# Chunk 0 of a fused scan and MLP kernel: state sums moved to other PSUM banks, halves copied first, two unused products on TensorE ahead of the sums

## The chip, the cores and the metric

The kernel runs on one core of a Trainium2 chip. The metric is the device time of one execution in microseconds, as the median over runs. A core has a matrix engine (TensorE, "PE" in the profile, its weight loads "PEld"), a vector engine (VectorE, "DVE"), a scalar engine (ScalarE, "ACT"), GpSimd ("POOL"), and SyncE ("SP"), which issues most DMAs. Each engine works through its own list of instructions in order and waits on semaphores for the others. PE writes its results to PSUM, here eight banks of 128 partitions x 512 float32 values; DVE and ACT read them there.

## The reference

Two computations follow each other. The first is a state-space scan over 4 batches, 8 heads and 768 tokens, with head size 32 and state size 16, here in chunks:

```python
cum = np.cumsum(la, axis=-1)                       # la = log(clip(a))
L = np.exp(cum[:, :, :, None] - cum[:, :, None, :]) * causal
M = np.einsum('bhin,bhjn->bhij', Cc, Bc) * L
y = einsum(M, xc) + einsum(Cc, state) * exp(cum)
state = exp(sum(la)) * state + sum_j(B_j x_j * exp(cum_last - cum_j))
```

The second takes y as 3072 tokens of 256 values and applies an MLP with a hard-swish: `h = y @ w_in` (256 x 2048), `g = h * clip(h + 3, 0, 6) / 6`, `out = g @ w_out` (2048 x 256). The weights come as float64 and are decoded to float32 on the chip.

## The kernel before, in words

**Tiling.** The 768 tokens are six chunks of 128 tokens; a chunk of all four batches is 512 columns of the MLP. Within a chunk the scan works in two halves of 64 tokens. `scores` (line 569) makes C·B for four pairs of heads, each pair q in its own bank `cb` (tags `f0` to `f3`). `multiply` (line 624) multiplies each pair by the decays `L` on DVE (line 637). `into_state` (line 592) makes the sums of B and x over a half: `sps[c][0]` for the first half, `sps[c][1]` for the second. `take` (line 620) copies the second one to `adds` on ACT; for chunk 0 the first one goes to `mid` on ACT, in two copies with a mask (line 632). `mix` (line 673) then makes y: for each half of the heads (u = 0, 1) products of x with `L` (line 685), and for chunk 0 behind each of them the products of `csT` with `mid` (line 556, `from_state`). `keep` (line 694) copies the four parts of y to `yT` on ACT, and `renew` (line 656) makes the next state from `mid` and `adds` on DVE.

**Banks.** `own_banks` (line 561) gives a chunk the two banks `y0` and `y1`. In each the first half of the columns is for y of the first 64 tokens, and the second half is for the sums. `own_halves` (line 665) gives y of the second 64 tokens two more banks, `f0` and `f1`. [...] In chunk 0 `d` (differences of sums of logs, lines 383 to 420) stands in `f0` to `f3` for chunk 0 itself, and for chunk 1 in two `o` banks and in `y0` and `y1`; ACT's exponentials (`diff_exp`, line 422) free them. `diff_mask` (line 385) puts a mask into these banks at the very start with products of up to 512 columns.

**Order.** The order on each engine is written out by hand (line 1155 on; no scheduler moves anything). For chunk 0: logs and differences, `scores(0)`, differences of chunk 1, `own_banks(0)`, `into_state(0, 0, 1)`, `multiply(0)`, `fade`, `mix(0)`, `keep(0)`. Between them stand steps that decode the first of four pieces of w_in (`weights(0, ..)`, lines 235 to 288, DVE and ACT). Loads of weight pieces (`load_w`, line 141) go into three `raw` buffers in turn. Piece 1 is issued by SP once DVE has written one element of its buffer; that write (line 154) stands in `multiply(0)` behind the second product of line 637. Piece 2 follows when piece 1 has landed (line 156). Later pieces wait for a buffer that has been decoded.

**The MLP of chunk 0.** From line 1210, `mlp_in` (line 706) makes 16 blocks of h, each 128 x 512, from two float32 products (line 711) in the banks `f0` to `f3` in turn. ACT makes the ramp (line 814), DVE multiplies it with h (line 819), which frees the bank. Decoding of the next weight pieces stands between these steps on ACT and DVE: block f uses piece f // 4 of w_in. `first_out` (line 822) then makes the output product with w_out, with chunk 1 of the scan in between.

Of the kernel before, what the change touches and what calls it, by code (L numbers as in the profile page):

```python
# [8 lines left out]
FP32 = mybir.dt.float32  # L9
# [12 lines left out]
def kernel(  # L22
# [24 lines left out]
    nc = tc.nc  # L47
    P = 128
    NB, NH, S, D = x.shape
    N = B.shape[-1]  # L50
    DM, DF = moe_w_in.shape[0], moe_w_out.shape[0]
    NC = S // P
# [6 lines left out]
    HT = P // 2  # L59
# [8 lines left out]
    ps = ctx.enter_context(tc.tile_pool(name="ps", bufs=1, space=PSUM))  # L68
# [17 lines left out]
    TURN = 2  # L86
# [54 lines left out]
    def load_w(i, queue=nc.sync):  # L141

        raw = loads.tile([P, NK * FP * 2 * P], U32, name="raw", bufs=NRAW)
        if i < NP:
            cols = slice(2 * i * FP * P, 2 * (i + 1) * FP * P)
            src = moe_w_in[:, cols].rearrange("(k p) f -> p k f", p=P)
            dst = raw.rearrange("p (k f) -> p k f", k=NK)
        else:
            r0 = (i - NP) * FP * P
            src = moe_w_out[r0:r0 + FP * P, :].rearrange("(k p) m -> p k m", p=P)  # L150
            dst = raw.rearrange("p (k m) -> p k m", k=FP)
        raws[i] = raw
        if i == 1:
            nc.vector.memset(raw[:, :1], 0)
        if i == 2:
            nc.gpsimd.tensor_copy(raw[:, :1], raws[1][:, :1])
        queue.dma_start(out=dst, in_=src)
# [6 lines left out]
    ident = const.tile([P, P], FP32, name="ident")  # L164
# [5 lines left out]
    def conceal_in(t, pattern):  # L170
# [23 lines left out]
        out=head, in_=head, pattern=[[-2 * N, NQ], [-N, 2]], compare_op=ALU.is_ge,  # L194
        fill=0.0, base=0, channel_multiplier=1)
    nc.gpsimd.affine_select(
        out=head, in_=head, pattern=[[2 * N, NQ], [N, 2]], compare_op=ALU.is_ge,
# [183 lines left out]
    ys, cbs, sps, adds = {}, {}, {}, {}  # L381
# [3 lines left out]
    def diff_mask(c, b):  # L385

        if c == 0:
            d = ps.tile([P, NH, HT], FP32, name="d", tag=f"f{b}")
        elif b < 2:
            d = ps_o.tile([P, NH, HT], FP32, name="d", tag="o")  # L390
        else:
            d = ps_y.tile([P, NH, HT], FP32, name="d", tag=f"y{b % 2}")
        n = NH if c else NH // (1 if b == 0 else 2 if b == 1 else 4)
        for h in range(0, NH, n):
            nc.tensor.matmul(
                out=d[:, h:h + n], lhsT=ident_h,
                rhs=hide.unsqueeze(1).to_broadcast([P, n, HT]), start=(h == 0), stop=True,
                skip_group_check=True)
        ds[c, b] = d
# [150 lines left out]
    def from_state(c, a, pairs=range(NQ)):  # L550

        csT, state = bTs[c][2], (mids[c] if a else states[c - 1])
        for b in range(NB):
            for q in pairs:
                pair, d0 = slice(32 * q, 32 * q + 32), 2 * D * (q % 2)
                nc.tensor.matmul(  # L556
                    out=ys[c][a, q // 2][d0:d0 + 2 * D, b], lhsT=state[pair, b],
                    rhs=csT[pair, b, HALF[a]], start=(a == 0 and b == 0), stop=True,
                    tile_position=(32 * q, d0), skip_group_check=True)

    def own_banks(c):

        both = [ps_y.tile([P, 2, NB, HT], FP32, name=f"y{u}", tag=f"y{u}") for u in range(2)]
        ys[c] = {(0, u): both[u][:, 0] for u in range(2)}
        sps[c] = [both[a if 0 < c < NC - 1 else 1 - a][:, 1] for a in range(2)]
        if c and c != TURN:
            from_state(c, 0)

    def scores(c):

        bT, cT, _ = bTs[c]
        cbs[c] = [ps.tile([P, NB, 2, HT], FP32, name="cb", tag=f"f{q}") for q in range(NQ)]
        if c not in ys and c:
            own_banks(c)
        for b in range(NB):
            for a, rows in enumerate(HALF):  # L580
                for q in range(NQ):
                    pair = slice(32 * q, 32 * q + 32)
                    nc.tensor.matmul(  # L583
                        out=cbs[c][q][rows, b], lhsT=bT[pair, b, rows],
                        rhs=cT[pair, b, :, rows], start=(b == 0), stop=True,
                        tile_position=(32 * q, a * HT), skip_group_check=True)
        if c == TURN:
            from_state(c, 0)
        if 0 < c <= TURN:
            into_state(c, *range(1 if c == TURN else 2))  # L590

    def into_state(c, *halves):
        xt, bs = xts[c], bss[c]
        own = c > TURN, c >= TURN
        if c > TURN:
            sps[c][0] = ps.tile([P, NB, 2 * D], FP32, name="sp", tag="f3")
        if c == 0:
            one = sps[c][0][:1, 0, :1]
            for left, right in ((ident_h[:, :1], hide[:, :1]), (bs[:, 0, :1], ident[:, :1])):
                nc.tensor.matmul(  # L600
                    out=one, lhsT=left, rhs=right, start=True, stop=True, skip_group_check=True)
        for b in range(NB):
            for q in range(NQ):
                hs = slice(b * NH + 2 * q, b * NH + 2 * q + 2)
                for a in halves:
                    nc.tensor.matmul(
                        out=sps[c][a][32 * q:32 * q + 32, b],
                        lhsT=bs[HALF[a], hs].rearrange("s h n -> s (h n)"),
                        rhs=xt[HALF[a], hs].rearrange("s h d -> s (h d)"),
                        start=(b == 0 and (c == 0 or own[a])), stop=True,  # L610
                        tile_position=(a * HT, 32 * q), skip_group_check=True)

    def new_state(t, sp, old):
        for u in range(2):
            ds_ = slice(u * D, (u + 1) * D)
            nc.vector.scalar_tensor_tensor(
                out=t[:, :, ds_], in0=sp[:, :, ds_], scalar=parity[:, u:u + 1],
                in1=old[:, :, ds_], op0=ALU.mult, op1=ALU.add)

    def take(c):  # L620
        adds[c] = att.tile([P, NB, 2 * D], FP32, name="adds", bufs=1)
        nc.scalar.copy(out=adds[c], in_=sps[c][1])

    def multiply(c):

        if c < TURN:
            take(c)
        if c <= TURN:
            mids[c] = mid = att.tile([P, NB, 2 * D], FP32, name="mid", bufs=1)
        if c == 0:  # L630
            for t in range(2):
                nc.scalar.activation(
                    mid[:, :, t * D:(t + 1) * D], sps[c][0][:, :, t * D:(t + 1) * D], AF.Copy,
                    scale=parity[:, t:t + 1])
        for q in (2, 0, 1, 3) if c >= TURN else range(NQ):
            hs = slice(2 * q, 2 * q + 2)
            nc.vector.tensor_tensor(
                out=Ls[c][:, :, hs], in0=Ls[c][:, :, hs], in1=cbs[c][q], op=ALU.mult)
            if c == 0 and q == 1:
                load_w(1)  # L640
            if 0 < c <= TURN and q == 1:
                new_state(mid, sps[c][0], tmps[c])
# [22 lines left out]
    def own_halves(c, more=0):  # L665

        for u in range(2):
            t = ps.tile([P, 1 + more * (1 - u), NB, HT], FP32, name="y2", tag=f"f{u}")
            ys[c][1, u] = t[:, 0]
            if u < more:  # L670
                ys[c]["more"] = t[:, 1]
# [176 lines left out]
    def weight_sums():  # L848


        t1 = w4[:, 0, 1]
        for n, p_, q_, op in ((3, lambda: w4[:, 1, 1], lambda: t1, ALU.subtract),
                              (2, lambda: wsums[3], lambda: w4[:, 0, 0], ALU.add),
                              (4, lambda: w4[:, 1, 0], lambda: wsums[2], ALU.subtract),
                              (1, lambda: t1, lambda: w4[:, 0, 0], ALU.subtract)):
            pool, tag = {1: (att, "yT"), 4: (const, f"w{NP - 1}")}.get(n, (const, f"t{n}"))
            wsums[n] = pool.tile([P, NJ, P], FP32, name=f"t{n}", tag=tag, bufs=1)
            nc.vector.tensor_tensor(out=wsums[n], in0=p_(), in1=q_(), op=op)
            yield
# [285 lines left out]
    def weights(i, n):  # L1145
        for _ in range(n):
            next(parts[i], None)
# [7 lines left out]
    for c in range(2):  # L1155
        for b in range(NB):
            diff_mask(c, b)
# [24 lines left out]
    for b in range(2, NB):  # L1182
        diff(1, b)
        diff_exp(1, b)
    weights(0, 2)
    own_banks(0)
    into_state(0, 0, 1)
    multiply(0)
    fade(0, HALF[1])
    weights(0, 1)  # L1190
# [16 lines left out]
    for k in range(NC):  # L1207
        gTs[k] = ffn.tile([P, NF, TB], FP32, name="gT")
        c, ahead = k + 1, k + 2
        if k == 0:  # L1210
# [16 lines left out]
            more, ins = weight_sums(), [in_parts(i) for i in range(NP)]  # L1227
# [101 lines left out]
        for i, _ in enumerate(wide_units(k)):  # L1329
# [18 lines left out]
            if c < NC:  # L1348
# [5 lines left out]
                u = {TURN: 7, TURN + 1: 7, TURN + 2: 5}.get(c, 5)  # L1354
# [49 lines left out]
```

## Time and profile before

| what | us |
|---|---|
| median of 3 runs (lowest, highest) | 338.85 (338.52, 339.15) |
| profiled execution, its own time | 339.71 |
| its span, first to last instruction | 338.0 |
| PE busy | 329.5 |
| DVE busy | 263.0 |
| ACT busy | 208.3 |
| POOL busy | 130.8 |
| mean granted TensorE clock | 0.990 of full |

The profile is of one execution. A row of the order of time gives start, length, engine, line, operation, output tile and inputs, form, and count; in brackets stands how long the engine was idle before it and what ended that. Rows of one line that follow each other are merged. A float32 product of PE shows as two records. "PEclk" and the clock column say which share of the full TensorE clock was granted.

### The profile page before, as it was taken

The numbers are of one execution on the slowest core, as the hardware profiler recorded it, in microseconds if no ns is written. First come the engines' busy times: TensorE is split into PE (matmuls) and PEld (weight loads), VectorE is DVE, ScalarE is ACT, GpSimd is POOL, SyncE is SP. The second block draws the span as 40 slices with busy tenths as digits, with TensorE's granted clock in tenths as the row PEclk, the third lists the DMA queues.
The fourth block names the chain that finished last, engine by engine and source line by source line (L and its number), as shares of the span: only waits on it lengthen the run. The fifth ranks groups of instructions, "written<-read, shape, count | busy, mean of one in ns | idle before, by whom it ended". The sixth has DMA issues, their size and how long they took to land.

```text
span 338.0 us, 8336 instructions
## 1 busy us (share of the span) xinstructions
PE 329.5 (97%) x3361; PEld 265.8 (79%) x3361; DVE 263.0 (78%) x419; ACT 208.3 (62%) x450; POOL 130.8 (39%) x126
## 2 busy tenths in 40 slices
PE   7799999999999999999999999999999999999995
PEld 3564448888868888888888888888888888899995
DVE  7778999879699729868959658947668958599974
ACT  3868887658985762587652478634488212677661
POOL 2100000162365699169984068781048750000000
PEclk9959999999999999999999999999999999999999
DMA  6769980492980206229207249100142001110001
GB/s 101 166 205 322 130 326 14 110 138 60 205 110 0 51 19 143 46 44 101 43 2 161 35 64 82 41 4 8 27 64 28 2 4 17 27 21 0 2 0 62
DMA packets 90278, 25.22 MB, mean 75 GB/s; under 512 B 82881, under 2 KB 86625, under 8 KB 89729
## 3 DMA queue, kind: packets, MB, share of 16 engines
q1 hardware_dynamic: 89664, 24.57, 38.5%
q8 instruction: 26, 0.43, 0.5%
q10 hardware_dynamic: 576, 0.13, 0.2%
q14 instruction: 12, 0.09, 0.1%
HBM read 21.33 MB, written 3.29 MB: 73 GB/s over the span
## 4 chain that ended last, share of the span: by engine, by line
PE 82%; DVE 6%; SPq 5%; ACT 2%; POOL 2%; DMA 2%; issue 1%; POOLq 0%
PE h L775 23%; PE h L711 9%; PE o L832 8%; PE wc L1023 7%; PE wb L1023 7%; PE o_end L987 6%; PE wa L1023 6%; SPq L1054 4%; PE wb L1031 3%; PE y L685 3%; PE y L556 2%; DVE q_part L915 2%; DVE gT L819 2%; DMA xt<-in_x_dram 2%; PE cb L583 2%
## 5 line engine op out<-in xcount | busy, mean ns | idle before, releaser
L819 DVE SCALAR_TENSOR_TENSOR gT<-gT,h 128x512 f32<-128x512 f32 x96 | 64.8, 684 | 24.4 <-ACT gT L814 22.9
L814 ACT ACTIVATE gT<-h,half 128x512 f32<-128x512 f32 x96 | 65.4, 686 | 21.8 <-PE h L775 21.2
L795 ACT ACTIVATE h<-h 128x512 f32<-128x512 f32 x66 | 38.3, 586 | 38.1 <-PE h L775 37.9
L775 PE MATMUL h<-y_hi,w_part 128*128 128x512 f32 x160 | 51.7, 408 | 0.6 <-DVE gT L819 0.5
L775 PE MATMUL h<-y_less,w_part 128*128 128x512 f32 x160 | 50.0, 399 | 0.0
L775 PE MATMUL h<-y_lo,w_part 128*128 128x512 f32 x160 | 49.5, 395 | 0.0
L878 POOL TENSOR_TENSOR s<-gT 128x512 f32<-128x512 f32 x16 | 24.9, 1556 | 51.1 <-DVE gT L819 51.1
L775 PEld LDWEIGHTS h<-y_hi,w_part 128*128 128x128 f32 x160 | 29.9, 188 | 7.9 <-DVE gT L819 1.5
L775 PEld LDWEIGHTS h<-y_lo,w_part 128*128 128x128 f32 x160 | 30.0, 188 | 7.3
L775 PEld LDWEIGHTS h<-y_less,w_part 128*128 128x128 f32 x160 | 29.1, 188 | 6.2 <-DVE h L792 0.3
L445 ACT ACTIVATE L<-L,cum_n 128x64 f32<-128x64 f32 x128 | 31.9, 339 | 2.2 <-POOL L L173 2.2
L711 PE MATMUL h<-yT,w_in 128*128 128x512 f32 x64 | 29.4, 622 | 0.0
L832 PE MATMUL o<-w_out,gT 128*128 128x256 f32 x128 | 28.8, 381 | 0.0
L832 PEld LDWEIGHTS o<-w_out,gT 128*128 128x128 f32 x128 | 24.1, 190 | 3.8 <-issue 0.5
L711 PEld LDWEIGHTS h<-yT,w_in 128*128 128x128 f32 x64 | 12.7, 201 | 16.0 <-issue 13.9
L878 POOL TENSOR_TENSOR gT<-gT 128x512 f32<-128x512 f32 x16 | 23.9, 1499 | 0.7
L173 POOL TENSOR_SCALAR_AFFINE_SELECT L<-L 64x1024 f32<-64x1024 f32 (+1 forms) x16 | 19.5, 1229 | 8.4 <-DMA L<-cum_d 8.1
L915 DVE TENSOR_TENSOR q_part<-gT,q_part 128x256 fp32r<-128x256 f32 x24 | 21.4, 922 | 0.0
L987 PE MATMUL o_end<-v_pair,g_pair 128*128 128x256 f32 x120 | 21.0, 281 | 0.0
L878 POOL TENSOR_TENSOR s<-s,gT 128x512 f32<-128x512 f32 x16 | 20.6, 1293 | 0.0
L987 PEld LDWEIGHTS o_end<-v_pair,g_pair 128*128 128x128 f32 x120 | 18.8, 189 | 1.2
L456 POOL TENSOR_TENSOR bs<-B,L 128x128 f32<-128x128 f32 x24 | 11.7, 504 | 18.7 <-ACT L L445 12.7
(170 smaller groups left out, 617.3 us busy)
## 6 DMA issues: line engine op xcount, KB each, us to landing
raw<-in_moe_w_in_dram SPq DMA_DIRECT2D x4, 1024.0 KB
raw<-in_moe_w_out_dram SPq DMA_DIRECT2D x4, 1024.0 KB
L<-cum_d SPq DMA_DIRECT2D x8, 512.0 KB
xt<-in_x_dram SPq DMA_DIRECT2D x6, 512.0 KB
out_dram<-back SPq DMA_DIRECT2D x128, 16.0 KB
B<-in_B_dram SPq DMA_DIRECT2D x6, 256.0 KB
eto<-cum_e SPq DMA_DIRECT2D x20, 64.0 KB
pairs<-in_C_dram SPq DMA_DIRECT2D x36, 32.0 KB
```

The lines of the kernel that those rows point to most:

```text
L173: nc.gpsimd.affine_select(out=t[rows], in_=t[rows], pattern=pattern, compare_op=ALU.is_ge, fill=-1e5, base=base, channel_multiplier=-1)
L445: nc.scalar.activation(Ls[c][:, b, h], Ls[c][:, b, h], AF.Exp, bias=cum_n[:, c, g:g + 1])
L711: nc.tensor.matmul(out=h[:, t:t + n], lhsT=w_in[f // FP][:, j, f % FP * P:(f % FP + 1) * P], rhs=yTs[k][:, j].rearrange("p b i -> p (b i)" ...
L775: nc.tensor.matmul(out=hs_[k, f], lhsT=w[j][:, f % FP * P:(f % FP + 1) * P], rhs=y[:, j], start=(start and j == 0), stop=True, skip_group_ ...
L795: nc.scalar.activation(h, h, AF.Copy, scale=1.0 / EPS + 1.0)
L814: nc.scalar.activation(gTs[k][:, f], h, AF.Relu, bias=half, scale=1.0 / 6.0)
L819: nc.vector.scalar_tensor_tensor(out=g, in0=g, scalar=1.0, in1=h, op0=ALU.min, op1=ALU.mult)
L832: nc.tensor.matmul(out=o[:, b % 2], lhsT=gTs[0][:, f, b * P:(b + 1) * P], rhs=w_out[:, f], start=(f == 0 and b % 2 == 0), stop=True, skip_ ...
L878: nc.gpsimd.tensor_tensor(out=o, in0=p_, in1=q_, op=op)
L915: nc.vector.tensor_tensor(out=l[:, j], in0=g[:, j], in1=h[:, j].bitcast(FP32), op=ALU.subtract)
L987: nc.tensor.matmul(out=ends_["cross" if n == 2 else "squares"][b], lhsT=g_parts[t][n][:, b * P:(b + 1) * P], rhs=w, start=(t == 0 and b < ...
L1023: nc.tensor.matmul(out=bank[:, slot], lhsT=lhs[:, j], rhs=rhs[:, j], start=(clear and j == 0), stop=True, skip_group_check=True)
```

## The change

In chunk 0 alone:

- The state sums go to two banks of their own, `f1` (first half) and `f0` (second half), which held `cb` of pairs 1 and 0. The banks `y0` and `y1` hold y alone.
- The y of the second 64 tokens goes to `f2` and `f3` in place of `f0` and `f1`.
- ACT copies the two masked halves of the first sum (`mid`) before the second sum (`adds`).
- Ahead of the sums, PE makes two float32 products of the identity with itself, repeated to 512 columns, into bank `y0`. Nothing reads them.
- At the start, the mask products of `diff_mask` for batches 2 and 3 of chunk 0 have 256 columns each in place of 128: four products in place of eight.

```diff
@@ diff_mask
-        n = NH if c else NH // (1 if b == 0 else 2 if b == 1 else 4)
+        n = NH if c else NH // (1 if b == 0 else 2)
@@ own_banks
-        sps[c] = [both[a if 0 < c < NC - 1 else 1 - a][:, 1] for a in range(2)]
+        if c:
+            sps[c] = [both[a if c < NC - 1 else 1 - a][:, 1] for a in range(2)]
+        else:
+            sps[c] = [ps.tile([P, NB, 2 * D], FP32, name="sp", tag=f"f{1 - a}") for a in range(2)]
         if c and c != TURN:
             from_state(c, 0)
+        return both[0].rearrange("p t b i -> p (t b i)")
@@ multiply
-        if c < TURN:
+        if 0 < c < TURN:
             take(c)
         if c <= TURN:
             mids[c] = mid = att.tile([P, NB, 2 * D], FP32, name="mid", bufs=1)
...
                     mid[:, :, t * D:(t + 1) * D], sps[c][0][:, :, t * D:(t + 1) * D], AF.Copy,
                     scale=parity[:, t:t + 1])
+            take(c)
@@ own_halves
-            t = ps.tile([P, 1 + more * (1 - u), NB, HT], FP32, name="y2", tag=f"f{u}")
+            t = ps.tile([P, 1 + more * (1 - u), NB, HT], FP32, name="y2", tag=f"f{u if c else 2 + u}")
@@ the order of chunk 0
-    own_banks(0)
+    free = own_banks(0)
+    for _ in range(2):
+        nc.tensor.matmul(
+            out=free, lhsT=ident, rhs=ident.unsqueeze(1).to_broadcast([P, NB, P]),
+            start=True, stop=True)
     into_state(0, 0, 1)
```

## The prediction

> **What bounds the kernel now.** I read the page first, then the chain of waits from 14 to 70 us, then stretches cut at the clock's steps, then the order of time on each engine.
>
> ```profile
> span 338.0 us, 8336 instructions
> PE 329.5 (97%) x3361; PEld 265.8 (79%) x3361; DVE 263.0 (78%) x419; ACT 208.3 (62%) x450; POOL 130.8 (39%) x126
> PEclk9959999999999999999999999999999999999999
> ```
>
> PE (TensorE) is busy for 97% of the span, so the time is PE's work plus its few holes. One digit of the clock row is not 9: the third slice (17 to 25 us), right where the change is made.
>
> ```profile
> 14.11 0.60 ACT L L425
> 16.93 0.27 ACT adds L622
> 17.24 0.96 PE y L685 x53
> 18.20 1.04 PE y L556 x16
> 19.24 1.11 PE y L685 x61
> 20.35 1.05 PE y L556 x16
> 21.40 29.31 PE h L711 x64
> 50.71 13.81 PE o L832 x64
> ```
>
> The chain of chunk 0: it runs on ACT (ScalarE) until 17.2 us, ending in the copy `adds`; then PE makes the second product y in four pieces (4.16 us) and, without a hole, the block product h.
>
> ```profile
> 11.04:14.45 3.41, 3.03 (x115) 2.22 (x115) 2.60 (x5) 2.10 (x3) 0.00 (x0) 1.00 1.24 159
> 14.45:17.86 3.41, 1.69 (x129) 1.43 (x130) 3.41 (x8) 3.23 (x6) 0.00 (x0) 1.00 0.37 68
> 17.86:21.28 3.42, 3.42 (x122) 2.90 (x104) 2.26 (x6) 1.12 (x3) 0.00 (x0) 0.50 0.61 246
> 21.28:24.69 3.41, 3.41 (x8) 1.51 (x5) 2.85 (x7) 3.21 (x6) 0.64 (x1) 0.50 0.48 127
> 24.69:28.10 3.41, 3.41 (x9) 1.52 (x8) 2.69 (x6) 2.33 (x4) 0.00 (x0) 1.00 1.02 400
> 29.03:36.50 7.47, 7.47 (x19) 3.34 (x18) 7.40 (x12) 6.19 (x8) 0.00 (x0) 1.00 1.17 202
> ```
>
> Columns: stretch and length, busy time of PE, weight loads, DVE (VectorE), ACT, POOL, then granted clock, DMA share, GB/s. The clock is halved from 17.86 to 24.69 us, two steps of 3.41 us. The 3.41 us before the drop hold 1.69 us of PE work; the 3.41 us before that hold 3.03, and the clock stayed. The last row: from 29.03 to 36.50 PE and DVE (7.40 of 7.47) are both full.
>
> **The change, part by part.** The rows it touches:
>
> ```profile
> 13.42 1.29 ACT L425 ACTIVATE L<-d 128x512 f32<-128x512 f32 x2 [0.47 <-PE d L417]
> 14.45 1.89 DVE L637 TENSOR_TENSOR L<-L,cb 128x512 f32<-128x512 f32 x3
> 15.54 0.86 PE L606 MATMUL y<-xt,bs 64*32 64x64 f32 x64 [0.57 <-DMA xt<-in_x_dram]
> 15.68 0.06 DVE L154 MEMSET raw<- 128x1 uint32 x1
> 15.78 7.08 SPq L157 DMA_DIRECT2D raw<-in_moe_w_in_dram  x3
> 15.78 1.15 ACT L273 ACTIVATE we<-we,bias_lo 128x1024 uint16<-128x1024 bf16 x1
> 16.25 0.68 DVE L637 TENSOR_TENSOR L<-L,cb 128x512 f32<-128x512 f32 x1
> 16.83 0.35 ACT L622 COPY adds<-y 128x256 f32<-128x256 f32 x1
> 17.09 0.63 ACT L632 ACTIVATE mid<-y,parity 128x128 f32<-128x128 f32 x2
> 17.90 1.22 DVE L287 SCALAR_TENSOR_TENSOR w_in<-wm,we 128x1024 f32<-128x1024 f32 x1
> ```
>
> *Masks at the start.* Eight mask products of 128 columns become four of 256: the same columns, back to back on PE either way. I take 0; it could be a few hundredths either way, hidden by PE's wait for x at 15.54.
>
> *Two idle products.* Each is 128x512 f32, the shape of an L711 product, which PE runs in two halves:
>
> ```profile
> 23.20 0.34 PEld L711 LDWEIGHTS h<-yT,w_in 128*128 128x128 f32 x1 [0.52 <-issue]
> 24.05 0.34 PEld L711 LDWEIGHTS h<-yT,w_in 128*128 128x128 f32 x1 [0.52 <-issue]
> 24.80 0.19 PEld L711 LDWEIGHTS h<-yT,w_in 128*128 128x128 f32 x1 [0.41 <-issue]
> 25.23 0.19 PEld L711 LDWEIGHTS h<-yT,w_in 128*128 128x128 f32 x1 [0.24 <-issue]
> ```
>
> Starts lie 0.85 us apart at half clock and 0.43 at full: one product is 0.86 us warm, two are 1.72. They write the bank that `diff_exp(1, 2)` frees at about 14.06 (the first half of the L425 row: 13.42 plus half of 1.29), so with the first weight load they last until about 15.95. Behind them on PE wait the two one-element products and the sums. Those started at 15.54, when x landed; now about 16.0, 0.46 later. Upper bound, if they run at half clock: 1.7 us more.
>
> *Sums in banks f1 and f0.* A new wait: these banks hold `cb` of pairs 0 and 1 until DVE's first two L637 products, done at 14.45 + 2 x 0.63 = 15.71 (third of 1.89 each). PE is still in the idle products then: 0. Gain: the first y product no longer shares a bank with the sums, so it needn't wait until `adds` has been copied (17.2); it follows the sums on PE at 16.0 + 0.86 = 16.86 instead of 17.24: 0.38 earlier. Its new banks f2 and f3 wait for the third and fourth L637 products; the fourth ends at 16.93, and the half that needs it comes 1.3 us after 16.86. 0.
>
> *Halves first.* ACT is in L273 until 16.93 either way. `mid` (0.63) now goes ahead of `adds` (0.35) and ends near 17.5, when the first quarter of y ends; `adds` then ends near 17.9, and its readers on DVE (`renew`) stand behind L287, which ends at 19.12. 0.
>
> *The clock.* From 14.45 to 17.86 PE would be busy nearly throughout (products until 15.95, sums, y): about 3.3 us against 1.69, more than the 3.03 that kept the clock. I take it that the clock stays. Then y costs, by halving 1.04, 1.11 and 1.05 and with 0.8 for the first piece (the sums, 64 halves of its form, took 0.86 with their end), about 2.4 us in place of 4.16: 1.75 less; h could start near 19.3 instead of 21.4. Its first block, four halves at 0.85, becomes four at 0.43: another 1.7 us. The clock is worth 3.45 us, and PE would be 3.8 us ahead.
>
> ```profile
> PE y L685 <- ACT adds L622: 0.8, 1, 0.8
> ```
>
> This is the longest of PE's holes there (from the waits: in total, times, longest). [...]
>
> *What is late next.* The lead is not kept. PE reuses four banks; block 8 of h needs block 4 multiplied by its ramp on DVE.
>
> ```profile
> 27.29 1.12 ACT L246 COPY ws<-raw 128x1024 uint16<-128x1024 uint16 x1 [1.05 <-DMA raw<-in_moe_w_in_dram]
> 29.03 0.69 DVE L819 SCALAR_TENSOR_TENSOR gT<-gT,h 128x512 f32<-128x512 f32 x1 [1.58 <-ACT gT L814]
> 35.23 1.27 DVE L819 SCALAR_TENSOR_TENSOR gT<-gT,h 128x512 f32<-128x512 f32 x2
> 36.82 0.19 PEld L711 LDWEIGHTS h<-yT,w_in 128*128 128x128 f32 x1 [0.24 <-issue]
> 42.03 1.49 DVE L819 SCALAR_TENSOR_TENSOR gT<-gT,h 128x512 f32<-128x512 f32 x2
> 47.89 1.22 DVE L287 SCALAR_TENSOR_TENSOR w_out<-wm,we 128x1024 f32<-128x1024 f32 x1
> 65.00 0.59 ACT L491 COPY bT<-t_ps 128x512 f32<-128x512 f32 x1 [2.02 <-PE t_ps L482]
> ```
>
> Block 1 starts at 24.80 and a block takes 4 x 0.43, so block 8 starts at 36.82. The L819 product of block 4 is the first of the two at 35.23 and ends at about 35.9: PE has 0.9 us in hand there. DVE got to 35.23 by its own full program since 29.03; that began when ACT had copied the third piece of w_in, whose DMA landed just before 27.29; that DMA follows the second piece's, which SP issued at 15.78 behind the memset at 15.68. Nothing of this row of causes moves with PE: the memset still stands behind the second L637 product. So in the new kernel block 8 starts no sooner than 35.95, however early y is: **the gain is 36.82 - 35.95 = 0.87 us**, and the other 2.9 us become PE holes before it (block 5 too must wait for the L819 of block 1, done at 29.03 + 0.69). The next places have more in hand: block 12 (24.80 + 44 x 0.43 = 43.7) against the first L819 at 42.03, done at 42.7: 0.96; the second matrix at 50.7 against L287's end at 49.11: 1.6. At 65.00 ACT waits for PE, and from there the other engines mostly follow PE, so the 0.87 us should reach the end.
>
> Sum: +0.46 (sums later) is covered by the old wait for `adds`, net -0.38 at y; clock -3.45; given back up to block 8 +2.96; total -0.87. The profiled execution took 339.71 us (span 338.0 and 1.7 around it), 0.86 more than the median of the runs, 338.85; I take the difference off the median: 338.85 - 0.87 = 337.98.
>
> **Rivals.**
>
> *The clock drops anyway.* If what counts is how much of the array works, the small y products weigh little: the stretch from 17.86 to 21.28 had PE busy throughout with them, and the clock didn't come back until 3.41 us of 128x512 products had followed. Against it: from 11.04 to 14.45 PE ran small products too, mixed with some 128x512 ones, and the clock stayed; the idle products are full size. Then y is 0.38 us earlier at half clock and that is worth half after 24.69: 0.19, 338.66.
>
> *The runs had no drop to lose.* If the clock's steps lie elsewhere in other executions, block 8 sits at 35.95 in both kernels: no gain, 338.85. For it: the unprofiled runs are 0.86 us faster than the profiled one, just the price of the drop. Against it: profiling may cost that itself, and the stretch from 14.1 to 17.2 is thin wherever a step falls. [...]
>
> *The third w_in piece lands later: slower.* With y earlier, the decode of the second piece, whose copies on ACT stand behind the last copy of y, starts about 0.5 us sooner, and so does the load of w_out that waits for its buffer:
>
> ```profile
> 24.78 0.37 SPq L157 DMA_DIRECT2D raw<-in_moe_w_out_dram  x1
> ```
>
> It would then share the DMA engines longer with the third piece, and that landing sets block 8 one for one. A landing 0.87 us later cancels the gain; 1.55 us later makes the kernel slower by over 0.2%. One MB at the 400 GB/s of the 24.69 row is 2.6 us, so a load served ahead would give 338.85 - 0.87 + 2.6 = 340.6. Against it: the third piece was issued long before, and only half a microsecond moves.
>
> **How the numbers follow.** A measurement of this kernel tells about 0.2% (0.68 us) from no change. Chances: the forecast 0.57, clock drops anyway 0.15, no drop in the runs 0.15, later landing or the like 0.13. The forecast's own range is 337.5 to 338.4: block 8 could gain up to 0.96 before block 12 binds, a step of the clock elsewhere makes the loss taken away smaller, and the three runs differ by 0.6. A fifth of it lies above 338.17, where "faster" ends. So faster 0.57 x 0.8 = 0.46; slower 0.14; same the rest, 0.40. For 8 in 10 the range takes in both cases of no gain and part of the later landing, and a margin below: 337.4 to 339.5.
>
> **What would show it.** Right: granted clock 1.00 throughout from 7.6 us; first y product right behind the sums near 16.9; h from about 19.3 at 0.43 us a half; new PE holes in h before blocks 4, 5 and 8 ended by DVE L819; block 8 near 35.95; `first_out` near 49.8. Wrong: a clock of 0.50 anywhere after 14 us; h without holes (then PE still bounds and the gain is other than 0.87); the third piece landing off 27.3; a lead of PE at 50 us that has gone by 65 or 100 us, with a new wait on ACT or POOL in its place.

## The result, and the profile after

The changed kernel took 337.72 us, the kernel before 339.08 us (medians of 13 runs each): a ratio of 0.9962, 95% interval 0.9947 to 0.9976. It is faster by 1.36 us. The prediction was 337.98 us, 0.87 us faster than the median it started from.

The page of the changed kernel, then the same stretches as before the change (length, busy PE, PEld, DVE, ACT, POOL, then granted clock, DMA share, GB/s):

```profile
span 336.2 us, 8336 instructions
PE 328.2 (98%) x3361; PEld 263.7 (78%) x3361; DVE 262.7 (78%) x419; ACT 207.8 (62%) x450; POOL 131.3 (39%) x126
PEclk9999999999999999999999999999999999999999
```

```profile
14.45:17.86 3.41, 3.34 (x150) 2.29 (x148) 3.38 (x8) 3.09 (x6) 0.00 (x0) 1.00 0.42 100
17.86:21.28 3.42, 3.42 (x90) 2.25 (x86) 2.50 (x5) 1.75 (x5) 0.54 (x1) 1.00 0.54 218
29.03:36.50 7.47, 6.85 (x15) 2.70 (x16) 7.37 (x13) 5.77 (x8) 0.00 (x0) 1.00 1.00 169
```

The dip of the clock is gone. PE is busy for 3.34 of the 3.41 us that held 1.69 before. And PE now has holes in the last stretch (6.85 of 7.47), where it had none, while DVE is as full as it was (7.37).

PE in order of time (start, length, engine, line, operation, count, in brackets the idle time before it and what ended it); L1193 is the idle products, L610 the sums, L690 and L556 y, L716 the blocks of h:

```profile
13.46 1.98 PE L1193 MATMUL y<-ident 128*128 128x512 f32 x4
15.42 0.16 PE L604 MATMUL sp<-hide,ident_h 128*1 128x1 bf16 x1
15.56 0.80 PE L610 MATMUL sp<-xt,bs 64*32 64x64 f32 x60
16.23 1.15 PE L690 MATMUL y<-L,xt 64*32 64x64 f32 x62
17.30 0.68 PE L556 MATMUL y<-csT,mid 32*64 32x64 f32 x16
17.91 0.86 PE L690 MATMUL y<-L,xt 64*32 64x64 f32 x64
18.70 0.68 PE L556 MATMUL y<-csT,mid 32*64 32x64 f32 x16
19.31 9.16 PE L716 MATMUL h<-yT,w_in 128*128 128x512 f32 x20
...
29.16 5.71 PE L716 MATMUL h<-yT,w_in 128*128 128x512 f32 x12 [0.69 <-DVE gT L824]
...
35.35 14.00 PE L716 MATMUL h<-yT,w_in 128*128 128x512 f32 x32 [0.48 <-DVE gT L824]
```

y follows the sums without a hole, h starts at 19.31 in place of 21.33, and PE then stops twice, ahead of blocks 5 and 8, for DVE's ramp product. The chain of waits shows the change of hands: where PE carried it from 17.2 us on, it now runs over three loads of w_in pieces, one behind the other, and over DVE and ACT until block 8 of h.

```profile
4.06 7.33 DMA raw<-in_moe_w_in_dram
...
14.09 0.14 DVE L L642
...
15.42 5.21 DMA raw<-in_moe_w_in_dram
...
20.75 0.65 POOL raw L156
21.40 0.02 issue
21.41 5.25 DMA raw<-in_moe_w_in_dram
...
26.69 1.11 ACT ws L246
...
35.35 14.00 PE h L716 x32
49.35 13.81 PE o L837 x64
```

### The profile page after: what moved, and what is told of

Its sections match the earlier page's. It is cut to its first block, busy times and chain, and to the rows that moved or that the text cites. A ratio compares the mean times of both kernels' runs of the same rounds, so it can differ in the third digit from the quotient of the medians.

```text
span 336.2 us, 8336 instructions
## 1 busy us (share of the span) xinstructions
PE 328.2 (98%) x3361; PEld 263.7 (78%) x3361; DVE 262.7 (78%) x419; ACT 207.8 (62%) x450; POOL 131.3 (39%) x126
## 3 DMA queue, kind: packets, MB, share of 16 engines
HBM read 21.33 MB, written 3.29 MB: 73 GB/s over the span
## 4 chain that ended last, share of the span: by engine, by line
PE 81%; DVE 8%; DMA 6%; ACT 2%; issue 1%; SPq 0%; POOL 0%; DVEq 0%; POOLq 0%
PE h L780 29%; PE wc L1028 8%; PE o L837 8%; PE wb L1028 8%; PE wa L1028 7%; PE o_end L992 6%; DMA raw<-in_moe_w_in_dram 5%; PE h L716 4%; PE wb L1036 3%; DVE gT L824 2%; PE y L690 2%; DVE q_part L920 2%; PE y L556 2%; PE cb L587 1%; DVE w_part L752 1%
## 5 line engine op out<-in xcount | busy, mean ns | idle before, releaser
L716 PE MATMUL h<-yT,w_in 128*128 128x512 f32 x64 | 28.8, 600 | 1.2 <-DVE gT L824 1.2
L716 PEld LDWEIGHTS h<-yT,w_in 128*128 128x128 f32 x64 | 11.6, 189 | 17.6 <-issue 11.5
```

Source lines behind the costliest of these rows:

```text
L716: nc.tensor.matmul(out=h[:, t:t + n], lhsT=w_in[f // FP][:, j, f % FP * P:(f % FP + 1) * P], rhs=yTs[k][:, j].rearrange("p b i -> p (b i)" ...
```

## The experiments

The runs come in three series, each on a chip of its own with the kernel before beside it; ratios are to that kernel in the same series, with 95% intervals. The kernel before had medians of 339.36 us in the first series (the first four kernels below, without the changed kernel itself), 338.78 in the second (`late_load_before`, the changed kernel again, one product, copy on DVE) and 339.38 in the third (four products, early write, both). Differences of a few tenths between kernels of different series are therefore not settled by their times. "Theory" is the author's own account, as it stood before each run.

**The two products alone.** The kernel before with

```diff
+    for _ in range(2):
+        nc.tensor.matmul(out=free, lhsT=ident, rhs=ident.unsqueeze(1).to_broadcast([P, NB, P]),
+            start=True, stop=True)
     into_state(0, 0, 1)
```

> The kernel before, with the two idle products alone ahead of the sums; banks, order of the copies and masks as before. Theory (the products hold the clock, and block 8 of h is bound by the landing of the third piece of w_in): granted clock 1.00 after 14 us; y starts as before when adds is copied (near 17.2 us), takes 2.5 us, h starts near 19.7 and block 8 waits for DVE all the same, so the whole gain of the change is here: about 337.8 us, ratio 0.996. Rival (the gain is from the new banks and the new order of the copies): no gain, 338.9 to 339.1 us.

Measured: 338.67 us, ratio 0.9977 (0.9963 to 0.9990), granted clock 0.998 or more in all nine runs. PE in order of time:

```profile
17.22 0.86 PE L686 MATMUL y<-L,xt 64*32 64x64 f32 x64 [0.46 <-ACT adds L623]
...
29.72 5.71 PE L712 MATMUL h<-yT,w_in 128*128 128x512 f32 x12 [0.83 <-DVE gT L820]
35.90 1.55 PE L712 MATMUL h<-yT,w_in 128*128 128x512 f32 x3 [0.47 <-DVE gT L820]
```

With the sums in the old banks y still waits for `adds` (0.46 us), and it makes no odds: block 8 waits for DVE all the same. In these nine runs the products were enough to hold the clock, and in the profiled one to reach that bound. The time is short of the expected 337.8 us (ratio 0.9977 in place of 0.996). In this execution the two loads behind the first took 5.42 and 5.41 us, against 5.21 and 5.25 in the changed kernel; whether the old banks have a part in that is not shown.

**Banks, order and masks without the products.** The changed kernel with

```diff
-    free = own_banks(0)
-    for _ in range(2):
...
+    own_banks(0)
```

> The changed kernel without the two idle products: new banks, halves first and fewer masks alone. Theory: y starts near 16.4 us, 0.8 earlier than before, but the clock drops to 0.50 at one of its steps after 16 us and stays there for 6.8 us; half of the 0.8 is left at block 8: 338.6 to 338.8 us. Rival (order and banks give the gain, the clock is kept because the hole ahead of y is gone): clock 1.00 throughout and 337.7 us.

Measured: 338.42 us, ratio 0.9974 (0.9962 to 0.9985). The granted clock was 0.998 or more in 8 of 12 runs, 0.983 to 0.995 in four. In the profiled execution it dropped for one step only:

```profile
12.76:16.17 3.41, 0.82 (x20) 0.53 (x20) 3.37 (x7) 3.16 (x5) 0.00 (x0) 1.00 0.52 50
16.17:19.59 3.42, 3.42 (x178) 3.13 (x177) 3.38 (x6) 2.01 (x6) 0.00 (x0) 0.50 0.72 208
```

```profile
16.03 0.16 PE L604 MATMUL sp<-hide,ident_h 128*1 128x1 bf16 x1 [2.59 <-DVE raw L154]
...
35.87 1.55 PE L716 MATMUL h<-yT,w_in 128*128 128x512 f32 x3 [0.47 <-DVE gT L824]
```

Half of each side's expectation fell. With the new banks and order the clock stayed in 8 of the 12 runs even without the products; why it did, with the hole below, was not tried. Where it dropped it cost time: the four runs took 338.71 to 339.38 us, the eight others 338.15 in the median. Only the mildest of the four (0.995) was profiled, and there the clock came back in time. The row at 16.03 shows what the products cover: the new banks make the sums wait until DVE has multiplied the second pair of `cb`, an idle time of 2.59 us. Block 8 waits for DVE at 35.9 both here and with the products alone. In this series the two took 338.42 and 338.67 us, and the next kernel, which has both parts, 338.44. So the two parts of the change do not add: either takes nearly the same gain, only that with the banks and the order alone the clock dropped in four of 12 runs.

**Mask products as before.** The changed kernel with

```diff
-        n = NH if c else NH // (1 if b == 0 else 2)
+        n = NH if c else NH // (1 if b == 0 else 2 if b == 1 else 4)
```

> The changed kernel with the eight mask products of 128 columns back. Theory: the same columns on PE, hidden by the wait for the split rows and for x; within 0.1 per cent of the changed kernel, 337.7 us. Rival (longer mask products warm the clock earlier): the clock reaches 1.00 a step of 3.41 us later and the time is 0.3 us or more above the changed kernel.

Measured: 338.44 us, ratio 0.9972 (0.9961 to 0.9983). The interval lies over that of the changed kernel, and from the first product of the decays to block 8 it takes 21.28 us here (14.46 to 35.74) against 21.26 there (14.09 to 35.35). No effect found, and the traces give no reason to expect one: in both kernels the first product of the decays starts 2.67 us after DVE's first decode step of w_in, which waits for a load and not for PE. The times alone don't settle it, since the changed kernel did not run in this series.

**The second piece of w_in issued later.** The changed kernel, and then the kernel before, with

```diff
-            if c == 0 and q == 1:
+            if c == 0 and q == 3:
                 load_w(1)
```

> The changed kernel with the one-element write that lets SP issue the second piece of w_in behind the fourth product of the decays in place of the second, 1.25 us later. Theory (block 8 hangs on the landings of the pieces, one for one): second and third piece land 1.25 us later, block 8 starts 1.25 us later (near 36.6 in place of 35.35), total about 1.2 us above the changed kernel, 338.9 us. Rival (PE or the free engines set block 8): less than 0.3 us above it.

Measured, in the changed kernel: 339.65 us, ratio 1.0008 (0.9996 to 1.0020), 1.2 us above the kernel with the masks as before in the same series. Its chain of waits:

```profile
14.36 0.14 DVE L L642
...
16.87 5.34 DMA raw<-in_moe_w_in_dram
...
23.00 5.39 DMA raw<-in_moe_w_in_dram
...
37.08 14.00 PE h L716 x32
```

From the first product of the decays to block 8 it is 22.72 us, 1.46 more than in the changed kernel: the two loads start later and block 8 follows. The write moved by 1.2 us; the rest is that the loads took 5.34 and 5.39 us here. This eats the whole gain.

> The kernel before, with the one-element write behind the fourth product of the decays, 1.25 us later. Theory (before, PE is behind by the cold clock and has 0.9 us in hand at block 8 in executions with two cold steps, 2.6 us with three): the pieces land 1.25 us later, and only 0 to 0.35 us of it shows, 338.9 to 339.7 us, against 1.2 us in the changed kernel. Rival (the landings set the time in both kernels): 1.2 us, 340.5 us.

Measured, in the kernel before: 339.43 us, ratio 1.0013 (1.0000 to 1.0026), some 0.4 us. Its chain, and the first use of the third piece:

```profile
16.89 0.27 ACT adds L622
17.16 0.04 issue
17.20 0.98 PE y L685 x53
...
21.39 29.29 PE h L711 x64
```

```profile
27.73 1.11 ACT L246 COPY ws<-raw 128x1024 uint16<-128x1024 uint16 x1 [1.49 <-DMA raw<-in_moe_w_in_dram]
```

The chain goes over `adds` and PE as it did, and h runs without a hole through the later landing. That landing is only 0.44 us later than in the profile before (27.73 against 27.29), mostly because the decays began 0.51 us earlier in this execution, so the trace shows less than the whole delay. The times show the rest: among runs with a clock of 0.988 to 0.990 the delay costs 0.34 us (medians 338.97 and 338.62), among those with 0.983 to 0.985 0.22 us (339.68 and 339.46), close to what the theory had. The same delay costs at least three times as much in the changed kernel: that is the change of bound, shown from both sides.

**The changed kernel again.** No edit, beside the next two kernels.

> The changed kernel itself, beside the next three on the same chip. Theory: 0.9 to 1.5 us under the kernel before, every run with a granted clock of 0.998 or more. If the eight narrow mask products cost something, it is clearly below their kernel's 338.44 us (0.3 us or more); if not, equal to it within 0.2 us.

Measured: 337.66 us, ratio 0.9965 (0.9951 to 0.9978); granted clock 0.998 or more in all ten runs, as in the 13 before. It is 0.78 us below the 338.44 of the kernel with the masks as before, which by the expectation's own measure speaks for a cost of the narrow masks. But the kernel before was 0.58 us lower here too, and the two ratios (0.9965 and 0.9972) have overlapping intervals: the times leave a cost of a few tenths open.

**One product in place of two.**

```diff
-    for _ in range(2):
+    for _ in range(1):
```

> The changed kernel with one idle product in place of two. Theory: what counts is how much of a 3.41 us stretch PE works; 0.86 us less of full-size work leaves a hole of about 0.8 us ahead of the sums, the clock drops in some executions and stays in others, and as a drop costs at most 0.3 us over the bound at block 8, the time is within 0.3 us of the changed kernel. Rival (any dense work there is enough): clock 0.998 or more in all runs.

Measured: 337.86 us, ratio 0.9975 (0.9963 to 0.9987), granted clock 0.998 or more in all 12 runs. A stretch of 3.41 us with the hole in it, and PE behind the product:

```profile
13.05:16.46 3.41, 2.40 (x90) 1.49 (x91) 3.38 (x8) 3.18 (x4) 0.00 (x0) 1.00 0.35 35
```

```profile
15.64 0.16 PE L604 MATMUL sp<-hide,ident_h 128*1 128x1 bf16 x1 [1.01 <-DVE raw L154]
```

The hole of 1.0 us is there, and the clock stayed each time, so the rival was right: in the profiled execution the clock stayed at 1.00 with 2.40 us of work in these 3.41, and one product did in all 12 runs. The second was not needed to keep the clock in them.

**Four products in place of two.**

```diff
-    for _ in range(2):
+    for _ in range(4):
```

> The changed kernel with four idle products in place of two. Theory: the two more delay the sums and y by 1.7 us (sums near 17.3 to 17.7, h near 21 to 21.4), but the lead of PE over the landings (near 3 us at block 4) covers it: block 8 starts where it did, and the time is within 0.2 us of the changed kernel (ratio to the kernel before 0.996 to 0.997). Rival (the products lie on the path): 1.7 us above the changed kernel, slower than before.

Measured: 338.42 us, ratio 0.9983 (0.9969 to 0.9997).

```profile
17.40 0.80 PE L610 MATMUL sp<-xt,bs 64*32 64x64 f32 x60
...
20.96 14.34 PE L716 MATMUL h<-yT,w_in 128*128 128x512 f32 x32
35.77 0.70 PE L716 MATMUL h<-yT,w_in 128*128 128x512 f32 x1 [0.47 <-DVE gT L824]
```

In the profiled execution the 1.7 us are covered as expected: h starts at 20.96, and block 8 waits for DVE at 35.77. But of the 12 runs four took 339.3 to 339.6 us, all with a clock of 0.998 or more, and the ratio is above the expected 0.996 to 0.997. So the expectation held in the profiled execution and not in all. None of the four was profiled, and what was late in them stays open.

**Shorter ways to the landings.** The changed kernel with the copy that holds back the third piece on DVE in place of POOL, behind the next state; with the second piece issued behind the first product of the decays; and with both:

```diff
-            nc.gpsimd.tensor_copy(raw[:, :1], raws[1][:, :1])
+            nc.vector.tensor_copy(raw[:, :1], raws[1][:, :1])
...
-    load_w(2)
-    load_w(3)
     renew(0)
     mix(0)
     keep(0)
+    load_w(2)
+    load_w(3)
```

```diff
-            if c == 0 and q == 1:
+            if c == 0 and q == 0:
                 load_w(1)
```

> The changed kernel with the one-element copy that holds back the third piece of w_in until the second has landed moved from POOL (0.65 us) to DVE (0.06 us), behind the next state. Theory (landings set block 8): third piece issued and landed 0.6 us sooner, block 8 and the end 0.6 us sooner, 0.5 to 0.6 us under the changed kernel. Rival (block 8 is then held by something else at once, DVE's own 9 us of work ahead of it or the second piece's decode): under 0.2 us.

> The changed kernel with the one-element write behind the first product of the decays in place of the second, 0.6 us earlier. Theory (block 8 follows the landings one for one, as the later write showed): 0.6 us under the changed kernel, ratio near 0.995. Rival (the second piece then shares the DMA engines with x, whose landing starts the sums): x lands later, no gain.

> The early write together with the copy on DVE. Theory: both savings add, 0.6 + 0.4 us under the changed kernel, ratio near 0.994 to 0.9935, the fastest of all. Rival (once the landings are 1 us sooner, DVE's and ACT's own work or the third and fourth pieces set block 8 and 12): no better than the copy on DVE alone, 0.9954.

Measured: copy on DVE 337.23 us, ratio 0.9954 (0.9937 to 0.9972), 0.43 us under the changed kernel in the same series; early write 337.76 us, 0.9957 (0.9945 to 0.9970); both 337.17 us, 0.9943 (0.9929 to 0.9957). The chain of waits of the kernel with both:

```profile
14.14 0.14 DVE L L642
...
14.86 5.53 DMA raw<-in_moe_w_in_dram
...
20.41 0.17 DVE raw L156
20.58 0.02 issue
20.59 5.48 DMA raw<-in_moe_w_in_dram
...
26.09 1.12 ACT ws L246
...
34.76 2.41 PE h L716 x5
```

From the first product of the decays to block 8: 21.26 and 21.15 us in the two profiles of the changed kernel, 20.90 with the copy on DVE (14.01 to 34.91), 20.75 with the early write (14.55 to 35.30), 20.62 with both. Each saving shows in this stretch, but less than its 0.6 us; with both, loads that took 5.2 us in the changed kernel took 5.5. In the time the copy on DVE shows. The early write alone was expected at a ratio near 0.995, and its 0.9957 can't be told from the 0.9962 and 0.9965 of the changed kernel, which did not run in its series. Its rival, that x lands later, did not come about: the sums waited for DVE's product, not for x. Both together has the lowest ratio of this study, with a median 2.2 us under the kernel before in its series (339.38).

## Why the prediction was right, and where its size was off

*The clock.* Right. All 23 runs of the changed kernel with a listed clock have 0.998 or more. The rival "the clock drops anyway" is out. In these two kernels the longest hole does not tell which of them keeps the clock: the kernel before lost it in the profiled execution with no hole over 0.84 us in the stretch ahead of the drop, and nearly every run of it has a lower clock (next point); the kernel with one product and a hole of 1.0 us kept it.

*The runs had no drop to lose.* Out as well: of 71 runs of the kernel before in the three series, 69 have a granted clock of 0.990 or less, two of 0.998 or more.

*y and h.* The start of h was put at 19.3 and came at 19.31. That is partly luck: terms on the way were off in opposite directions. The products began at 13.46, not 14.06, since in this execution the differences ahead of them were done earlier (its first two products of line 408, from 6.57 us, took 0.38 and 0.39 us, those of the kernel before, from 6.76, 0.63 and 0.60). The sums, put behind the products at 16.0, began at 15.56, and y at 16.15 in place of 16.86. Against these 0.7 us, y took 3.16 us and not 2.4. Its first piece, put at 0.8, took 1.15. The others had been halved; at full clock a piece of 16 products with `mid` took 0.61 us where halving gave 0.52, and the second piece of 64 with `L` 0.79 where it gave 0.56. The wait of the sums for DVE's second product of the decays had been put at nothing. In this execution the two end together (DVE's write behind that product at 15.38, the idle products at 15.44); with the masks as before, where the decays began later, the sums waited 0.30 us for it, and without the products it is the wait that counts.

*The lead given back at block 8.* Right, and the main point: the holes in h ahead of blocks 5 and 8, ended by DVE, and a gain much below PE's lead. The later write and the earlier one move block 8 the way they move the landings; in the kernel before the later write hardly shows. What is gained at block 8 also reaches the end, as predicted: in the eleven profiled executions in which block 8 waits for DVE, the time from its start to the end of the run is 302.3 to 303.1 us, in the kernel before 302.9.

*The size.* Put at 0.87, measured 1.36. The step that was mis-sized is the loss taken away: it was read from one execution with two cold steps (3.41 us each at a clock of 0.50; mean 0.990). The runs of the kernel before fall into two groups. 33 have a clock of 0.988 to 0.990 and a median of 338.68 us; 36 have 0.983 to 0.985 and a median of 339.54. By an estimate from the mean clock the second group has three cold steps: a mean of 0.984 over some 337 us takes about 11 us at half clock, three times 3.41. Against the first group in its own series (338.62) the changed kernel is 0.96 us faster (337.66): the 0.87 holds for executions like the one profiled. The other half of the runs is slower still, by 0.86 us over all and by 0.65 to 0.84 within a series, and that is gained too. Why a third cold step would cost less than 0.9 us and not the 1.7 us that it takes from PE was not tried; no execution of that group was profiled.

In the two profiled executions block 8 is 1.47 us earlier (36.82 to 35.35), not 0.87. The other 0.6 us comes from loads of w_in, which the change does not touch. The two later loads took 5.21 and 5.25 us in place of some 5.4 and 5.3, and DVE's first product of the decays stands at 14.09 in place of 14.45. That start has a cause which the prediction did not follow back: DVE decodes the first piece of w_in before the decays, and waits for it to land. Before and after:

```profile
11.78 0.69 DVE L249 TENSOR_SCALAR wm<-raw 128x1024 uint32<-128x1024 uint32 x1 [0.78 <-DMA raw<-in_moe_w_in_dram]
```

```profile
11.42 0.69 DVE L249 TENSOR_SCALAR wm<-raw 128x1024 uint32<-128x1024 uint32 x1 [1.04 <-DMA raw<-in_moe_w_in_dram]
```

In all 13 profiled executions the first product of the decays stands 2.66 to 2.67 us behind this row, and the row itself lies anywhere from 11.25 to 12.04 us, although the load is issued near 4.1 each time. So in the changed kernel the bound is a chain of three loads, and block 8 moves with the landing of the first, which differs by up to 0.8 us between executions. What makes it vary was not tried.

*A later landing.* The landing did not slip, so this rival did not come about; that it would count about one for one the later write shows.

*The masks.* Put at 0. The traces show nothing, and the times leave a few tenths of a us open.

## What to carry to other kernels

Ask of a gain at one engine what it will wait for next, and read that wait's time in hand before adding up: here a lead on PE put at 3.8 us was worth 0.9 us, and either half of the change would have brought most of it. Follow the new wait back to its first cause as well: here it was a load issued near 4.1 us, some 9 us ahead of the idle products. When a bound changes hands, small things on the new chain begin to count: a 0.65 us copy that merely held back a DMA was off the chain before and worth 0.4 us after. And where the clock's state differs between executions, one profile shows one of them; look at the granted clock of all runs before pricing it.

## What the runs showed of the hardware that was not expected

- The records of the granted clock begin, with 1.00, at 5.06 us in the profile of the changed kernel and at 7.62 in that of the kernel before. In the kernel before a product of line 408 took 0.63 us ahead of that time (at 6.76) and 0.38 to 0.39 behind it; in the changed kernel those from 6.57 on took 0.38 to 0.39.
- In the kernel before the 3.41 us ahead of the drop held 1.69 us of PE work (14.45 to 17.86), in the kernel without the idle products 0.82 (12.76 to 16.17). In two profiled executions without a drop there were stretches of that length with 2.40 us (one product, 13.05 to 16.46) and 2.22 us (the later write in the changed kernel, 24.88 to 28.29; mean clock 1.000, though one of that kernel's 12 runs has 0.993). In the kernel before a stretch at clock 0.50 that was filled with products of 64x64 and 32x64 operands (17.86 to 21.28) was followed by another at 0.50; in the kernel without the idle products one filled with sums and y (16.17 to 19.59) was not: 16 products of line 556 took 1.11 us in it, at 18.18, and 0.68 behind it, at 20.15. What tells the two apart was not tried.
